# Later token groups of 512 by a quarter of the features, with block products of 256 columns, in a fused retention and feed-forward kernel

## The chip, the cores and the metric

One NeuronCore of a Trainium2 chip. The metric is the device time of one launch in microseconds (us), median over runs. All data is float32 except the two weight matrices, which arrive as float64 bit patterns and are converted on the core.

## What is computed

The reference, cut to what matters:

```python
# q, k, v: (4, 8, 768, 64); w_in: (512, 2048); w_out: (2048, 512)
for t in range(S):                                   # retention, per batch and head
    state = gamma * state + outer(k[t], v[t])
    y[t] = (q[t] @ state) / sqrt(D)
x = y.transpose(0, 2, 1, 3).reshape(3072, 512)
h = x @ w_in
sp = np.maximum(h, 0.0) + np.log1p(np.exp(-np.abs(h)))   # softplus
g = h * erf(sp)
out = g @ w_out                                      # (3072, 512)
```

## The kernel before

The order of all work is written out by hand in one Python function; every engine executes its own instructions in that order, and waits on semaphores where an operand or a buffer is not ready.

**Retention.** The 3072 tokens are 24 chunks j of 128 tokens (6 per batch). `load(j)` issues a chunk's DMAs on the SP queue: one for k, 16 small ones that put q into blocks of 32 by 32, 16 more that put k into such blocks (`kb`, `load_blocks`, L187), one for v. `prepared(j)` scales k, `kb` and q on VectorE (DVE) and transposes the blocks on DVE into `kT` and `qT`, in five steps. `sub_visit(j, g)` does the chunk's matmuls on TensorE (PE): scores against the masked keys, values, state, and the update of `state`; it writes the chunk's columns of `xT`. The pool `loads` has three buffers for `kq` and `v`, two for `kb`.

**First 512 tokens.** For these (g = 0 to 3, `G0` is 4) the hidden layer is computed plainly in groups of 512 tokens by 512 features while the weights are being loaded and converted (`weights`, `conversion`).

**Later groups.** From g = 4 to 23 the tokens go in pieces of 256, each with two groups of half the features. The first of them, `hidden_plain`, multiplies plainly. The other 19 use a fast block scheme for the hidden layer: x and `w_in` are cut into 4 blocks along the inner dimension, x into 2 blocks of 128 tokens, `w_in` into blocks of 256 features (4 per half); 26 products (`STEPS`) of sums of blocks give the 8 output blocks. The sums of x are made by 18 DVE additions (`x_sums`), the sums of `w_in` once per half by 30 DVE additions (`W_SUMS`, `sum_in`). `hidden_steps` executes a product as two matmuls of 128 columns (tokens), L951, into one of four PSUM banks, which the next steps use again in turn; each of 26 reads adds a bank into the output `h` in SBUF, the first write of a block by a copy on ScalarE (ACT), L965 and L967, the rest by DVE, L963.

The gate: softplus on ACT (`gate_softplus`), erf on ACT (`gate_erf`, another table), product with `h` on DVE (`gated`). The second layer uses a fast scheme of seven products (`project_part`, parts 1 to 7, L1034; four sums of `e` blocks, `g_sums`; sums of `w_out` blocks, `sums`, made by an ACT copy and an accumulating DMA from the POOL queue, L352 and L353). Its accumulators in four PSUM tiles `o0` to `o3` add up over the two groups of a token piece, and `put_part` then combines them into `r` and writes 256 rows of the output.

**Order within a later group.** During the 26 steps of group g, three parts of the second layer of group g-1 are put among them; after them stand softplus, a chunk's visit, the x sums of the next piece, `load(j+3)`, erf, four more parts of g-1, and the gate:

```python
        for n, _ in enumerate(hidden_steps(g), start=1):
            ...
            if n in (14, 18, 24):
                project_part(g - 1, {14: 1, 18: 2, 24: 4}[n])
        ...
            if even:
                all_of(prepared(j + 2))
            if j + 3 < NJ:
                load(j + 3)
            j += 1
        gate_erf(g)
        for p in (5, 6, 7, 3):
            project_part(g - 1, p)
```

Of the kernel before, what the change touches and what calls it, by code (L numbers as in the profile page):

```python
# [45 lines left out]
W_SUMS = (  # L46
    (16, 2, 6, "+"),
    (17, 8, 10, "-"),
    (4, 4, 17, "+"),
    (10, 10, 16, "+"),  # L50
    (18, 16, 4, "-"),
    (19, 18, 5, "-"),
    (20, 1, 19, "-"),
    (20, 0, 20, "+"),
    (21, 9, 20, "+"),
    (9, 13, 9, "-"),
    (22, 15, 13, "-"),
    (23, 15, 9, "-"),
    (7, 3, 7, "+"),
    (24, 20, 12, "-"),  # L60
    (25, 18, 7, "+"),
    (2, 2, 3, "+"),
    (8, 12, 8, "-"),
    (12, 17, 12, "-"),
    (3, 3, 15, "-"),
    (15, 2, 15, "-"),
    (19, 19, 13, "-"),
    (16, 16, 7, "+"),
    (7, 7, 10, "+"),
    (4, 4, 6, "-"),  # L70
    (1, 1, 5, "+"),
    (5, 5, 2, "+"),
    (6, 14, 12, "+"),
    (6, 6, 15, "-"),
    (13, 23, 11, "-"),
# [61 lines left out]
def kernel(  # L137
# [29 lines left out]
    loads = ctx.enter_context(tc.tile_pool(name="loads", bufs=3))  # L167
# [24 lines left out]
    def load(j):  # L192
        b, c = divmod(j, NC)
        if j == JPC - 1:

            x = act.tile([P, N], F32, name="e", bufs=1)
            KQ[j] = x[:, : 2 * d_model].rearrange("p (i h d) -> p i h d", i=2, h=H)
            V[j] = x[:, 2 * d_model : 3 * d_model].rearrange("p (h d) -> p h d", h=H)
        else:
            KQ[j] = loads.tile([P, 2, H, D], F32, name="kq")  # L200
            V[j] = loads.tile([P, H, D], F32, name="v")
        now = slice(c * C, (c + 1) * C)
        if j >= NB:
            KB[j] = loads.tile([P, HP * C], F32, name="kb", bufs=2)
            nc.sync.dma_start(KQ[j][:, 0], k[b, :, now, :].rearrange("h p d -> p h d"))
            load_blocks(KQ[j][:, 1].rearrange("p h d -> p (h d)"), q[b, :, now, :])
            load_blocks(KB[j], k[b, :, now, :])
# [14 lines left out]
    w_in_sb = const.tile([P, 2, N_W, 2 * P], F32, name="w_in_sb")  # L222
    w_out_sb = const.tile([P, 2, 7, FG, DH], F32, name="w_out_sb")

    def w_in_of(ft, kk):
        half, s, i = ft // (2 * FG), ft % (2 * FG) // FG, ft % FG
        return w_in_sb[:, s, 4 * (2 * half + i // 2) + kk, i % 2 * P : (i % 2 + 1) * P]

    def w_out_of(ft):
        half, s, i = ft // (2 * FG), ft % (2 * FG) // FG, ft % FG  # L230
        return w_out_sb[:, s, 2 * half : 2 * half + 2, i, :]
# [3 lines left out]
    CE = 2 * d_model  # L235
    spare = [w_out_sb[:, s, 4:7].rearrange("p a b c -> p (a b c)") for s in range(2)]
    spare += [w_in_sb[:, s, 16:24].rearrange("p a f -> p (a f)") for s in (1, 0)]
    raws = [x[:, : 2 * CE].bitcast(I64) for x in spare]

    def halves(x):  # L240
        return x.rearrange("p (h c) -> p h c", h=2).bitcast(U32)

    numbers = halves(spare[0][:, 2 * CE :])
    later = ret.tile([P, N_X, P], F32, name="xs", bufs=1)[:, : CE // P].rearrange("p a f -> p (a f)")
    powers = [halves(spare[1][:, 2 * CE :]), halves(later)]
    last_power = halves(spare[1][:, :CE])
# [38 lines left out]
    def conversion(n):  # L285
# [4 lines left out]
        half, s, at = i // 4, i % 4 // 2, i % 2  # L290
# [3 lines left out]
            range(2) if n < 4 else (None,), (slice(1), slice(1, 2)) if n == 0 else (slice(None),)  # L294
        )
        for part, rows in parts:
            last = n > 0 or rows.start == 1
            words = raws[place[n]].bitcast(U32)
            if which == "in":
                f = slice(2 * P) if part is None else slice(part * P, (part + 1) * P)  # L300
                fb = 2 * half + at
                to = w_in_sb[:, s, 4 * fb : 4 * fb + 4, f].rearrange("p (h k) f -> p h k f", h=2)
            else:
                to = w_out_sb[:, s, 2 * half : 2 * half + 2, at * 2 : at * 2 + 2, :]
            words = words.rearrange("p (h a b w) -> p h a b w", h=2, a=2, w=2)
            number, power = (
                x.rearrange("p h (q a b) -> p q h a b", q=1 if part is None else 2, a=2)[:, part or 0]
                for x in (numbers, last_power if n == n_p - 1 else powers[n % 2])
            )
            if part is not None:  # L310
                words, number, power, to = words[:, rows, :, f], number[:, rows], power[:, rows], to[:, rows]
# [26 lines left out]
    in_sums = [0, 0]  # L338

    def sum_in(s, upto):  # L340

        assert all(("hidden", 2 * FG + s * FG + u) in done for u in range(FG))
        for to, a, b, sign in W_SUMS[in_sums[s] : upto]:
            nc.vector.tensor_tensor(w_in_sb[:, s, to], w_in_sb[:, s, a], w_in_sb[:, s, b], op=OP[sign])
        in_sums[s] = max(in_sums[s], upto)

    def sums(s):

        assert ("project", s) in done
        x = {name: w_out_sb[:, s, at] for name, at in OUT.items()}  # L350
        for to, a, b in (("T1", "12", "11"), ("T2", "22", "T1"), ("T3", "22", "12"), ("T4", "21", "T2")):
            nc.scalar.activation(x[to], x[b], AF.Copy, scale=-1.0)  # L352
            nc.gpsimd.dma_start(x[to], x[a], accum_op=ALU.add)  # L353
            done.add((to, s))
# [17 lines left out]
    def later_sums():  # L372
        for s in range(2):
            yield from sums(s)
# [13 lines left out]
    def need(*what):  # L388
        nonlocal room
        while what not in done:  # L390
            if next(weight_steps, done) is done:
                next(last_steps)
# [38 lines left out]
    state_2 = loads.tile([P, HP * C], F32, name="kb", bufs=2)[:, : HP * D]  # L431
    state_2 = state_2.rearrange("p (u d) -> p u d", d=D)
    mid = [state, state_1, state_2, state, None, state_1]
    adds_of = {JPC: range(2), JPC + 1: range(1), JPC + 2: range(1)}
# [131 lines left out]
    def ret_mask(j):  # L566
        AM[j] = ret.tile([P, 2, HP, C], F32, name="am")
# [64 lines left out]
    def sub_mask(j):  # L632
        AM[j] = ret.tile([P, 2, HP, C], F32, name="am")
        for s in range(2):
            nc.vector.tensor_tensor(
                AM[j][:, s, :, :D],
# [30 lines left out]
    def sub_results(j):  # L667
# [4 lines left out]
        pp = [ret_psum() for _ in range(2)]  # L672
        for a in range(2):
            t, before = slice(a * D, (a + 1) * D), mid[2 * (j - JPC) + a]
            for u in PAIRS:
                for r in range(2):
# [3 lines left out]
                        start=(a == 0 and u % 2 == 0), stop=False, skip_group_check=True,  # L680
                    )

        for crossed in range(2):
            for u in PAIRS:
                for a in range(2):
# [6 lines left out]
                        AM[j][t, r, u, :D],  # L692
                        start=False, stop=True, skip_group_check=True,
                    )
        for r in range(2):
            nc.scalar.copy(XC[m][:, r::2, i * C : (i + 1) * C], pp[r][:, :2, :])
# [3 lines left out]
    def sub_sums(j):  # L700
        m, i = divmod(j, JPC)
        for r in range(2):
            a = 1 - r
            x = XC[m][:, r::2, i * C + a * D : i * C + (a + 1) * D]
            nc.vector.tensor_tensor(x, x, SC[j][a][:, 2:, :D], op=ALU.add)
# [7 lines left out]
    def sub_visit(j, g):  # L713
# [16 lines left out]
        def of_state(a):  # L730
            t = slice(a * D, (a + 1) * D)
            for u in PAIRS:
                for r in range(2):
                    col, own = u // 2, slice(r * D, (r + 1) * D)
                    x = state_1 if g == G0 else state
                    nc.tensor.matmul(  # L736
                        pp[r][col * D : (col + 1) * D, u % 2, t], x[own, u, :], QT[j][own, u, t],
# [7 lines left out]
        def of_values(crossed):  # L745
            for u in PAIRS:
                for a in range(2):
# [6 lines left out]
                        AM[j][t, r, u, :D],  # L754
# [5 lines left out]
        last = chunk_of(g - 1)  # L760
        if (g - G0) % 2 == 1:
            clear.update((("o", 0), ("o", 1)))
        new = [
            None if g == G0 else O[last][3][:, 1, :].rearrange("p (u d) -> p u d", d=D),
            pp[1][:, 2:, :].rearrange("p a (b d) -> p (a b) d", d=D),
        ]
        adds = range(int(g == G0), 2 if c < NC - 1 else 1)
# [8 lines left out]
        if g > G0 and c:  # L776
            nc.vector.tensor_tensor(state, state, new[0], op=ALU.add)
        elif g > G0:
# [17 lines left out]
        if c < NC - 1:  # L796
            nc.vector.tensor_tensor(state, state_1 if g == G0 else state, new[1], op=ALU.add)
# [12 lines left out]
    HS, E, O = {}, {}, {}  # L810

    def gate_softplus(g):


        name = "r" if g < 4 and g % 2 else "e"
        E[g] = act.tile([P, N], F32, name=name, bufs=1)
        nc.scalar.activation(E[g], HS[g], AF.Softplus)  # L817
# [6 lines left out]

    def gate_erf(g):

# [512 lines left out]
```

## Time and profile before

| what | value |
|---|---|
| time, three runs | median 663.42 us (663.25 to 664.19) |
| profiled execution | 663.2 us, of which the recorded span is 661.5 us |
| PE matmul busy | 655.3 us, 6200 instructions |
| PE weight loads busy | 556.6 us |
| DVE busy | 508.4 us, 1101 instructions |
| ACT busy | 280.1 us, 402 instructions |
| POOL busy | 11.5 us, 29 instructions |
| mean granted TensorE clock | 0.999 of full speed |
| first stretch, weights and first 512 tokens | to about 127.5 us |
| one later group, table load to table load (L1256) | 25.92 us, for instance 400.82 to 426.74 |

The profile is of one execution. Matmuls are pipelined, so their recorded lengths overlap; the distance of their starts is what they cost. Each float32 matmul appears as two passes with a weight load (PEld) each. DVE, ACT and POOL execute one instruction after another, and the distance of starts in a row is a little less than an instruction's recorded length. SPq and POOLq rows are the issuing of DMAs, not the transfers.

### The profile page before, as it was taken

How to read it: one execution, taken by the hardware profiler on the slowest of the kernel's cores; microseconds unless marked ns; L12 is line 12 of the kernel's file. 1: busy time of each engine (PE TensorE's matmuls, PEld its weight loads, DVE VectorE, ACT ScalarE, POOL GpSimd, SP SyncE). 2: the span in 40 equal slices, each digit the busy share in tenths (PEclk: the TensorE clock that was granted, in tenths of full speed). 3: DMA queues.
4: the chain of work that ended last, by engine and by line, in shares of the span. 5: the costliest groups of instructions: out<-in, count | busy, mean ns of one | idle time of the engine just before them, and what ended most of it. 6: DMA issues, size and time to landing. Idle time of an engine off the chain costs nothing.

```text
span 661.5 us, 15245 instructions
## 1 busy us (share of the span) xinstructions
PE 655.3 (99%) x6200; PEld 556.6 (84%) x6200; DVE 508.4 (77%) x1101; ACT 280.1 (42%) x402; POOL 11.5 (2%) x29
## 2 busy tenths in 40 slices
PE   8999999999999999999999999999999999999998
PEld 7744444576999999999999999999999999999997
DVE  5999999969986886787678678677787788476464
ACT  3468363445535334244254253342432442542440
POOL 1000000110100000000000000000000000000000
PEclk9999999999999999999999999999999999999999
DMA  9999944385753321222222322222231210000001
GB/s 189 222 244 212 247 130 106 63 152 91 145 122 61 85 46 34 66 47 46 69 45 47 73 40 47 61 51 43 41 75 35 45 54 1 2 34 0 1 33 33
DMA packets 159414, 51.90 MB, mean 78 GB/s; under 512 B 143216, under 2 KB 149744, under 8 KB 159344
## 3 DMA queue, kind: packets, MB, share of 16 engines
q1 hardware_dynamic: 157776, 46.72, 32.9%
q0 software_dynamic: 1152, 4.19, 3.3%
q8 instruction: 49, 0.80, 0.5%
q14 instruction: 21, 0.17, 0.1%
q10 hardware_dynamic: 416, 0.01, 0.0%
HBM read 40.39 MB, written 6.29 MB: 71 GB/s over the span
## 4 chain that ended last, share of the span: by engine, by line
PE 98%; DMA 1%; DVE 0%; SPq 0%; ACT 0%; issue 0%
PE o L1034 37%; PE hp L951 22%; PE r L951 12%; PE hp L860 8%; PE o L896 8%; PE hp L980 2%; PE r L736 2%; PE hp L628 1%; PE o L772 1%; DMA kq<-in_k_dram 1%; PE r L557 1%; PE o L604 1%; PE r L751 1%; PE hp L751 1%; PE r L524 1%; PE r L772 0%
## 5 line engine op out<-in xcount | busy, mean ns | idle before, releaser
L1034 PE MATMUL o<-w_out_sb,h 128*128 128x256 f32 (+1 forms) x648 | 143.8, 379 | 0.4 <-DVE r L1294 0.4
L951 PE MATMUL hp<-xs,w_in_sb 128*128 128x128 f32 x988 | 138.1, 275 | 0.0
L1034 PEld LDWEIGHTS o<-w_out_sb,h 128*128 128x128 f32 x648 | 120.5, 190 | 17.1 <-DVE r L1294 0.6
L963 DVE TENSOR_TENSOR h<-h,hp 128x256 f32<-128x256 f32 x190 | 78.0, 419 | 70.2 <-PE hp L951 65.4
L951 PEld LDWEIGHTS hp<-xs,w_in_sb 128*128 128x128 f32 x988 | 128.4, 192 | 2.9
L1034 PE MATMUL o<-w_out_sb,e 128*128 128x256 f32 x480 | 113.5, 379 | 0.0
L1034 PEld LDWEIGHTS o<-w_out_sb,e 128*128 128x128 f32 x480 | 86.8, 190 | 9.4
L817 ACT ACTIVATE e<-h 128x2048 f32<-128x2048 f32 x22 | 42.1, 1911 | 119.8 <-DVE h L963 119.7
L963 DVE TENSOR_TENSOR h<-h,r 128x256 f32<-128x256 f32 x152 | 56.9, 416 | 22.3 <-PE r L951 21.4
L965 ACT COPY h<-hp 128x256 f32<-128x256 f32 x38 | 14.2, 373 | 130.8 <-PE hp L951 102.6
L951 PE MATMUL r<-xs,w_in_sb 128*128 128x128 f32 x456 | 63.3, 275 | 0.0
L951 PEld LDWEIGHTS r<-xs,w_in_sb 128*128 128x128 f32 x456 | 57.0, 192 | 0.0
L860 PE MATMUL hp<-xT,w_in_sb 128*128 128x512 f32 (+2 forms) x144 | 56.5, 548 | 0.0
L849 DVE TENSOR_TENSOR e<-h,e 128x1024 f32<-128x1024 f32 x42 | 49.3, 1214 | 8.0 <-ACT e L830 8.0
L860 PEld LDWEIGHTS hp<-xT,w_in_sb 128*128 128x128 f32 x144 | 25.7, 190 | 27.0 <-issue 24.4
L951 PE MATMUL hp<-xT,w_in_sb 128*128 128x128 f32 x304 | 46.3, 275 | 0.0
L951 PEld LDWEIGHTS hp<-xT,w_in_sb 128*128 128x128 f32 x304 | 41.5, 192 | 1.4 <-issue 0.5
L830 ACT ACTIVATE e<-e 128x2048 f32<-128x2048 f32 (+1 forms) x23 | 42.1, 1836 | 0.2
L967 ACT ACTIVATE h<-hp 128x256 f32<-128x256 f32 x57 | 21.8, 383 | 29.6 <-PE hp L951 28.3
L951 PE MATMUL r<-xT,w_in_sb 128*128 128x128 f32 x228 | 31.7, 275 | 0.0
L830 ACT ACT_TABLE_LOAD x24 | 30.8, 1283 | 0.4
L951 PEld LDWEIGHTS r<-xT,w_in_sb 128*128 128x128 f32 x228 | 28.5, 192 | 0.0
(160 smaller groups left out, 794.8 us busy)
## 6 DMA issues: line engine op xcount, KB each, us to landing
w_out_sb<-in_moe_w_out_dram SPq DMA_DIRECT2D x14, 512.0 KB, 5.8
kq<-in_k_dram SPq DMA_DIRECT2D x23, 256.0 KB, 4.2
v<-in_v_dram SPq DMA_DIRECT2D x23, 256.0 KB, 3.5
out_dram<-r SPq DMA_DIRECT2D x23, 256.0 KB, 2.4
kq<-in_q_dram SPq DMA_DIRECT2D x288, 16.0 KB, 1.8
kb<-in_k_dram SPq DMA_DIRECT2D x288, 16.0 KB, 1.7
w_in_sb<-in_moe_w_in_dram SPq DMA_DIRECT2D x8, 512.0 KB, 12.4
w_out_sb<-w_out_sb POOLq DMA_DIRECT2D x8, 512.0 KB, 5.2
```

The lines of the kernel that those rows point to most:

```text
L736: nc.tensor.matmul(pp[r][col * D : (col + 1) * D, u % 2, t], x[own, u, :], QT[j][own, u, t], start=first(r, col), stop=True, skip_group_ch ...
L751: nc.tensor.matmul(other[a][own, u % 2, D:] if crossed else pp[a][own, u % 2, t], V[j][t, 2 * u + r, :], AM[j][t, r, u, :D], start=crossed ...
L817: nc.scalar.activation(E[g], HS[g], AF.Softplus)
L830: nc.scalar.activation(E[g][:, half], E[g][:, half], AF.Erf)
L849: nc.vector.tensor_tensor(E[g][:, half], HS[g][:, half], E[g][:, half], op=ALU.mult)
L860: nc.tensor.matmul(HP_[ft][:, t], w_in_of(ft, kk), XC[0][:, kk, t], start=(kk == 0), stop=(kk == n_k - 1),)
L896: nc.tensor.matmul(O[0][tt].rearrange("p (d c) -> p d c", d=2), E[g][:, u * TCH + tt * P : u * TCH + (tt + 1) * P], w_out_of(ft), start=(f ...
L951: nc.tensor.matmul(to[:, u, :], w_in_sb[:, s, w, u * P : (u + 1) * P], XS[m](x), start=first and u == 0, stop=True, skip_group_check=True,)
L963: nc.vector.tensor_tensor(h, h, of, op=ALU.add if plus else ALU.subtract)
L965: nc.scalar.copy(h, of)
L967: nc.scalar.activation(h, of, AF.Copy, scale=-1.0)
L1034: nc.tensor.matmul(O[m][i][:, half, at], G[g][a][:, u * P : (u + 1) * P], w_out_sb[:, s, OUT[b], u, at], start=i not in started, stop=(s = ...
```

## The change

Later groups become 512 tokens by a quarter of the features (512): 20 groups again (g = 4 to 23), four for each of the five blocks of 512 tokens. A product of the block scheme is one matmul with 256 tokens as its columns and 128 features as its rows; the first later group uses the scheme too, and `hidden_plain` is gone. The weights are laid out by quarters; the 30 sums of `w_in` are made four times, for the first quarter on DVE (`sum_in`), for the other three by ACT copies and accumulating DMAs from POOL (`sums_in`), put between other work by `some(1)` after every odd step, and what is left of the next quarter's sums is put out at the end of a group. The order of `W_SUMS` is another one.

The second layer of a group goes in two pairs of 128-token blocks (`pairs`, in alternating order): the first pair among the steps of the next group, the second between that group's visit and the next group's steps. The accumulators of a pair are drained after one or two groups (`results`), five times per block, and what is not the first write of its rows is added into the output in DRAM by an accumulating DMA from POOL; for one pair of the last block an SBUF tile collects the parts. Gate, softplus and erf go by pairs too.

To make room in SBUF, `loads` has two buffers instead of three, the load after a visit is `load(j+2)` instead of `load(j+3)`, and several tiles of the first stretch share memory with `e_all` and `xs`. Chunks 6 and 7 are handled ahead of the first later group, chunks 8 to 23 by visits, one in each of the first 16 groups.

The diff, cut to its core:

```diff
-    loads = ctx.enter_context(tc.tile_pool(name="loads", bufs=3))
+    loads = ctx.enter_context(tc.tile_pool(name="loads", bufs=2))
...
+    def sums_in(q):
+
+        ready_to_sum(q)
+        for to, a, b, sign in W_SUMS:
+            if to == a and sign == "-":
+                nc.vector.tensor_tensor(w_in_at(q, to), w_in_at(q, a), w_in_at(q, b), op=OP[sign])
+            else:
+                if sign == "-" or to not in (a, b):
+                    nc.scalar.activation(w_in_at(q, to), w_in_at(q, b), AF.Copy, scale=float(sign + "1"))
+                    b = a
+                elif to == b:
+                    b = a
+                nc.gpsimd.dma_start(w_in_at(q, to), w_in_at(q, b), accum_op=ALU.add)
+            in_sums[q] += 1
+            yield
...
     def later_sums():
-        for s in range(2):
-            yield from sums(s)
+        yield from sums_in(1)
+        yield from sums(0)
+        yield from sums_in(2)
+        yield from sums(1)
+        yield from sums_in(3)
...
         for w, x, bank, first, reads in STEPS:
-            to = banks[bank]
-            for u in range(2):
-                nc.tensor.matmul(
-                    to[:, u, :],
-                    w_in_sb[:, s, w, u * P : (u + 1) * P],
-                    XS[m](x),
-                    start=first and u == 0,
-                    stop=True,
-                    skip_group_check=True,
-                )
-            of = to[:, :2].rearrange("p u t -> p (u t)")
+            to = banks[bank][:, :SCH]
+            nc.tensor.matmul(to, w_in_at(q, w), XS[m](x), start=first, stop=True, skip_group_check=True)
+            of = to.rearrange("p (h c) -> p h c", h=2)
...
+    def results(g, pair):
+
+        m = block_of(g)
+        t0 = m * TCH + pair * SCH
+        r = act.tile([P, 8, DH], F32, name="r", bufs=1)
+        nc.scalar.copy(r[:, 7], OP_[pair][3][:, 0])
+        yield
+        nc.vector.tensor_tensor(
+            r[:, 0:5:4], OP_[pair][0], r[:, 7:8].to_broadcast([P, 2, DH]), op=ALU.add
+        )
+        yield
+        o57 = OP_[pair][1]
+        nc.vector.tensor_tensor(
+            r[:, 5:7], o57, r[:, 4:5].to_broadcast([P, 2, DH]), op=ALU.add
+        )
+        nc.vector.tensor_tensor(r[:, 3], r[:, 6], o57[:, 0], op=ALU.add)
+        yield
+        nc.vector.tensor_tensor(r[:, 1:3], r[:, 5:7], OP_[pair][2], op=ALU.add)
...
+            if t0 in written_out:
+                nc.gpsimd.dma_start(rows, x, accum_op=ALU.add)
+            else:
+                nc.sync.dma_start(rows, x)
...
+    sub_states(j + 1)
+    sum_in(0, len(W_SUMS) // 2)
+    project(G0 - 1, 1)
+    put_first(0)
+    some(4)
+    sub_results(j + 1)
+    sub_sums(j + 1)
+    x_sums(1)
+    load(j + 3)
+    sum_in(0, len(W_SUMS))
+    project(G0 - 1, 2)
+    put_first(1)
...
+    gate_softplus(G0)
+    project(G0 - 1, 3)
+    put_first(2)
+    sub_visit(j, ps_o.tile([P, 2, DH], F32, name="o0"))
+    put_first(3)
+    load(j + 2)
...
     for g in range(G0 + 1, NG):
...
+        next_chunk = prepared(j + 1) if more else none()
+        order = {
+            1: (next_chunk,), 2: (gated_x, late), 3: (gated_x,), 4: (next_chunk, late), 5: (late,), 6: (next_chunk, late),
+            7: (gated_y, late), 8: (next_chunk,), 9: (gated_y,), 10: (next_chunk,),
+            11: (sums_x,), 12: (sums_x,), 13: (sums_x,), 14: (sums_x,),
+            18: (sums_y,), 20: (sums_y,), 22: (sums_y,), 24: (sums_y,),
+        }
+        parts = {14: (1,), 16: (2,), 18: (4, 6), 20: (5,), 22: (7,), 24: (3,)}
+        drains = {15: 1, 19: 1, 23: 1, 25: 1}
         for n, _ in enumerate(hidden_steps(g), start=1):
             for steps in order.get(n, ()):
                 next(steps, None)
+            for p in parts.get(n, ()):
+                project_part(before, x, p)
+            if n in drains:
+                if n == 15:
+                    bank = OP_[x][3]
+                next(drain, None)
+            if n % 2:
+                some(1)
...
+        if g + 1 < NG and quarter(g + 1):
+            while in_sums[quarter(g + 1)] < len(W_SUMS):
+                next(last_steps)
 
         nc.scalar.activation(idle, idle, AF.Softplus)
-        gate_softplus(g)
+        gate_softplus(g, x)
         if more:
-            sub_visit(j, g)
+            sub_visit(j, bank)
+            if j + 2 < NJ:
+                load(j + 2)
             j += 1
+        for p in (1, 2, 4):
+            project_part(before, y, p)
+        gate_softplus(g, y)
+        if g + 1 < NG and quarter(g + 1) == 0:
+            x_sums(block_of(g + 1))
+        for p in (6, 5, 7, 3):
+            project_part(before, y, p)
+        if at == FG - 1:
+            late = results(before, y)
+        if g < NG - 1:
+            for pair in pairs(g):
+                gate_erf(g, pair)
```

In the texts below, group 0 is the first later group (g = 4), group 1 the next, up to group 19; a link is one step of a chain of dependent weight sums.

## The prediction

> **What bounds the kernel now.** First the page: engine shares and the chain that ended last.
>
> ```profile
> span 661.5 us, 15245 instructions
> ...
> PE 655.3 (99%) x6200; PEld 556.6 (84%) x6200; DVE 508.4 (77%) x1101; ACT 280.1 (42%) x402; POOL 11.5 (2%) x29
> ...
> PE 98%; DMA 1%; DVE 0%; SPq 0%; ACT 0%; issue 0%
> ```
>
> TensorE is the bound from end to end, and nobody makes it wait. So two questions decide: is its own work less afterwards, and does anything begin to hold it up? Second, the timeline of a later group (columns: start, length, engine, line, operation).
>
> ```profile
> 425.26 0.61 PE L951 MATMUL hp<-xs,w_in_sb 128*128 128x128 f32 x4
> ...
> 425.71 0.61 PE L951 MATMUL hp<-xT,w_in_sb 128*128 128x128 f32 x4
> ...
> 434.17 0.46 PE L736 MATMUL r<-qT,state 64*64 64x64 f32 x16
> ...
> 447.90 0.69 DVE L537 TENSOR_TENSOR kq<-kq,kq_s 128x512 f32<-128x512 f32 x1
> ...
> 448.50 1.41 DVE L963 TENSOR_TENSOR h<-h,r 128x256 f32<-128x256 f32 x4
> ...
> 449.45 1.89 PE L1034 MATMUL o<-w_out_sb,e 128*128 128x256 f32 x8
> ...
> 451.18 0.61 PE L951 MATMUL hp<-xs,w_in_sb 128*128 128x128 f32 x4
> ```
>
> The profile counts two passes per matmul. Take starts, not lengths: four 128-column passes start every 0.445 us, 0.111 each; eight 256-column passes take 451.18-449.45 = 1.73, 0.2165 each. Twice 0.111 is 0.222: PE is limited by columns, and 256 columns in one instruction save 0.006 us of 0.222. DVE in a row: four 256-column additions in 1.41 us, 0.335 each with the last at its full 0.42; the 512-column step starts 0.60 before the next; 128 columns take 0.21 (five of L933 in 1.10).
>
> Third, the SP queue in that group, the sizes and landings on the page, and the accumulating DMA of the second-layer weights.
>
> ```profile
> 435.12 0.39 SPq L205 DMA_DIRECT2D kq<-in_k_dram  x1
> 435.56 9.01 SPq L187 DMA_DIRECT2D kq<-in_q_dram  x16
> 444.62 7.54 SPq L187 DMA_DIRECT2D kb<-in_k_dram  x16
> ```
>
> ```profile
> kb<-in_k_dram SPq DMA_DIRECT2D x288, 16.0 KB, 1.7
> ...
> w_out_sb<-w_out_sb POOLq DMA_DIRECT2D x8, 512.0 KB, 5.2
> ```
>
> ```profile
> 164.61 0.85 POOL L353 DMA_DIRECT2D w_out_sb<-w_out_sb  x1 [10.06 <-ACT w_out_sb L352]
> ...
> 170.44 2.01 ACT L352 ACTIVATE w_out_sb<-w_out_sb 128x1024 f32<-128x1024 f32 x2 [2.68 <-DMA w_out_sb<-w_out_sb]
> ```
>
> One chunk's load starts 0.96 us after the last block product (434.16) and its last `kb` piece is issued at 452.16: landed at 453.9, 19.7 us after that product. The accumulating DMA holds its follower 170.44-164.61 = 5.8 us.
>
> **TensorE's own work.** Removed: 19 groups x 104 passes x 0.1113 = 219.9, and `hidden_plain`, 64 x 0.2165 = 13.9. Added: 20 x 52 x 0.2165 = 225.2. Second layer: 56 passes a group on both sides. Sum -8.6 us. The Trainium skill (Perfetto Trace Analysis, Matmuls) says larger matmuls are more efficient when possible; its TensorE: Matmul & The Clock Gate (Back-to-back issue gap) gives sustained spacings of 81 ns at 128 columns and 131 at 512, by which 256 columns would cost far less than two of 128 and the block products nearly halve, an estimate of some -90 us. The two starts above decide against it: 0.2165 against 0.222.
>
> **The load of a chunk.** Before, with three buffers, `load(j+3)` follows the visit of chunk j, and the chunk is scaled more than a group later. Now two buffers, `load(j+2)` after the visit, and `prepared(j+1)` of the next group's block products wants that very chunk. The built program's DVE order in a group is: k scale, two 512-column gates, `kb` scale, then the first addition into h (step 5). The `kb` scale waits for all 16 pieces. From the end of a group's block products (0): visit 2.0, seven parts of the second pair 28 x 0.2165 = 6.06, so step 1 could start at 8.06 and step 5's result is there at 10.4. `kb` lands at 19.7. Steps 1 to 8 run; step 9 needs bank 0 again, which the addition of step 5, queued behind the `kb` scale, reads at 20.3; step 9 starts at 20.8 instead of 11.5: 9.3 lost. Then DVE has, from the `kb` scale to the addition of step 13, six 512-column steps (3.65) and ten of 256 columns (9 x 0.335 + 0.42), so bank 0 is free for step 15 only at 26.85; PE lacks another 2.6 on the way there. From there 12 steps x 0.433 and 6 parts x 0.866 = 10.4: the group ends at 37.2. Without waits it is 25.4; before, the table loads of L1256 stand 25.92 apart. Lost: 11.9 a group. In the second quarter of a block the left-over drain puts 2.13 us of DVE work into the same stretch: 14.0. This meets groups 4 to 14 (eight regular, three with the drain): 95 + 42 = 137 us. Group 3 is loaded during an earlier stall and loses only the DVE part, 2.3; the last five, without chunks, 4.7.
>
> The price's ends: if the pieces land at 17, 9.2 a group; if the drain of SP is as in the slowest load (383.34 to 401.1), 12.7.
>
> **PE's clock.** In the stretch from 658.0 to 661.5, where PE does 0.64 us of work, the granted clock reads 0.80; nothing longer is seen. A wait of 9 us may thus lower it. TensorE: Matmul & The Clock Gate (What's actually happening) puts the idle clock at half after about 3.4 us, for about as long; by it an estimate of 1.7 us a group; no run here shows it. By the rows: were steps 9 to 13 (5 x 0.433) to take twice as long, the 2.2 us would fit into the 2.6 that PE then waits for DVE anyway. I take 0, and 11 x 2.2 = +24 as the upper end.
>
> **Weight sums by DMA.** Quarter 0 costs DVE 30 x 0.21. Quarters 1 to 3 each become 25 accumulating 64 KB DMAs, 16 ACT copies and 5 DVE steps. For such a DMA the trace has no row: lower end 0.85 + 1.7 (POOL step and 16 KB landing) = 2.55, upper end the 5.8 of 512 KB; I take 3.2, nearer the small end, as 64 KB is an eighth (out_dram: 64 KB lands in 1.6, 256 KB in 2.4). DMA: Bandwidth & Descriptors (Anatomy of one DMA) states 2.0 us plus bytes/436e3, an estimate of 2.15; no row here has that size. With 0.27 per ACT copy and 0.3 to POOL, the longest dependent chain of the 30 sums is 37 us; from sum 8 to the end 30, from 14 to the end 23. ACT and DVE take their queues in order, so whatever stands behind a waiting copy waits too:
> - Start. `prepared(7)` waits for chunk 7's `kb` (135.9 + 1.7 = 137.6); four DVE steps, masks, 15 sums, `x_sums` (18 x 0.335 = 6.0), 5 sums end at 153.9. PE's own work (from 127.5: two begins and two results at 1.1, three parts at 3.5) ends at 142.4: 11.5.
> - Group 0: block-product copies behind copies of quarter 1: 3.4. Then the four second-layer sums with two 5.8 us links hold ACT: first copy at 165, two links of 7.2 (1.06 + 0.3 + 5.8), last copy, table and softplus 1.06 + 1.28 + 1.91 end at 183.7, the copies into `xT` behind them let group 1 start at 185.8 instead of 174.5: 11.3.
> - Group 1: its chunk's load stands on SP behind `put_first(3)`, starts at 186.5, lands at 205.2; step 9 at 206.3: 19.7 with the first waits. At its end 16 sums of quarter 2 are put out at once ahead of softplus, and their last DVE steps ahead of the visit's state addition: sum 8 is issued at step 15, the chain ends 30.2 later and the state addition 0.7 after it, while PE comes to wait for that state 10.4 + 1.8 after step 15: 19.
> - Group 2: four second-layer sums among the first steps hold ACT (step 8 starts at 9.7 instead of 3.0, step 14 at 16.9 instead of 5.6; part of it is waited for anyway): 9.8. At its end 21 sums of quarter 3 at once, the state at 54.2 from the group's start, PE waiting for it at 31.4: 22.8.
> Sum 97.5 (with 2.55 per DMA 83, with 5.8 about 140).
>
> **The rest.** Five drains per block instead of two: 15 more x 2.13 us of DVE, in the stretches above. Additions into DRAM on POOL: two per drain, 26 in all at 0.85; the buffer `r` comes round 20 us later at the soonest, so they are hidden (if not, ACT's first drain copy waits for up to 5.8). The end: 84 passes instead of 88, but the last pair is gated after the first: +1.
>
> **Sum.** 663.2 (the profiled execution; span 661.5, median of the runs 663.42) - 8.6 + 97.5 + 2.3 + 137 + 4.7 + 1 = 897; I say 895.
>
> **Rivals.**
> 1. The load does not bind: `kb` lands before 10 us, or DVE's queue is not blocked by it. Then regular groups lose DVE's own crowding, 2.3 (drain 4.2, `x_sums` 3.6): 41 in all, and the start and the sums some 75: 770. For it: before, DVE waits for `kb` once only, 3.0 us. Against: that load has a group more time.
> 2. Everything added is hidden, and only PE's columns count: 663.2 - 8.6 = 655, faster. It decides if SP gives a chunk's 32 pieces in under 9 us (16.6 above) and a DMA link costs under 1 us. DVE's 77% leaves room on average, but a wait in order is no matter of averages.
> 3. Slower still: DMA links of 5 us and a halved clock after each wait: 940 and more.
> The change does what it says: the built program has 520 block products of 256 columns.
>
> **Numbers.** Forecast 0.66 (its own range 840 to 945), rival 1 and what lies between it and the forecast 0.22, rival 2 0.05, rival 3 0.07. About 0.2% is what a measurement can tell from no change. Range 770 to 945: it leaves out rival 2, most of 3 and the low tail of 1. Faster 0.04, same 0.01, slower 0.95.
>
> **What would show it.** Right: table loads about 37 us apart in groups 4 to 14 and 26 in the last ones; DVE waiting about 10 us a group for `kb`'s DMA; PE waiting for DVE's addition into h; two PE holes of about 20 us at the ends of groups 1 and 2 with ACT and DVE waiting for `w_in` DMAs; 256-column passes 0.2165 apart. Wrong: `kb` waits under 3 us a group, or PE at 98% of the chain.

## The result and the profile after

| | median, us | range |
|---|---|---|
| before | 663.42 | 663.25 to 664.19 |
| after, four runs | 915.81 | 913.56 to 916.64 |

The changed kernel takes 1.3796 times as long (95% interval 1.3768 to 1.3823). The forecast was 895, its own range 840 to 945. The profiled execution took 913.56 us, 250.4 us more than that of before; its page opens so:

```profile
span 911.9 us, 13667 instructions
...
PE 704.0 (77%) x5196; PEld 543.9 (60%) x5196; DVE 536.3 (59%) x1200; ACT 297.5 (33%) x501; POOL 102.2 (11%) x130
...
PE 35%; SPq 20%; DVE 16%; DMA 13%; issue 11%; ACT 3%; POOL 2%; DVEq 0%; ACTq 0%; POOLq 0%
```

Nothing is busy four fifths of the time, so waits, not work, set the time: the chain that was PE's at 98% now runs a fifth of its length through the issuing of DMAs on SP. The waits (engine, line, what for: us in total, times, longest) name the places:

```profile
PE hp L1006 <- DVE h L1012: 131.5, 27, 13.4
DVE kb L584 <- DMA kb<-in_k_dram: 123.0, 13, 11.9
...
PE r L785 <- DVE state L823: 37.1, 2, 21.2
```

The first two lines are in the main one and the same stall, seen from two engines: DVE waits for the pieces of `kb` (L584), and PE for the addition into `h` (L1012) that stands behind that step in DVE's queue. The third line is the two holes ahead of the state additions. Next the timeline of group 10:

```profile
569.35 7.87 SPq L187 DMA_DIRECT2D kq<-in_q_dram  x16
577.26 7.54 SPq L187 DMA_DIRECT2D kb<-in_k_dram  x16
...
577.45 0.60 PE L1006 MATMUL r<-xT,w_in_sb 128*128 128x256 f32 x2
...
586.27 0.69 DVE L584 TENSOR_TENSOR kb<-kb,kq_b 128x512 f32<-128x512 f32 x1 [10.34 <-DMA kb<-in_k_dram]
586.88 0.41 DVE L1012 TENSOR_TENSOR h<-h,hp 128x256 f32<-128x256 f32 x1
...
587.35 2.08 PE L1006 MATMUL hp<-xs,w_in_sb 128*128 128x256 f32 x4 [9.30 <-DVE h L1012]
...
593.33 0.70 PE L1006 MATMUL hp<-xs,w_in_sb 128*128 128x256 f32 x2
```

The block products of the group before ended at 566.1. From there: `kb` is scaled at 20.2 (forecast: landing at 19.7), step 8 is the row at 577.45, step 9 starts at 21.2 (20.8), step 15 at 27.2 (26.85). PE's wait is 9.30, the forecast 9.3.

Behind the wait, too, the four passes of the row at 587.35 take 2.08 us, about twice 1.03, which four take elsewhere in the group: the granted clock reads 0.50 from 587.3 to 589.2 and 1.00 again from 593.3 on. Where the 250.4 us arose follows from the starts of the softplus tables, one per group (L1321 after, L1256 before):

| stretch | before | after | more | forecast, with its share of the -8.6 |
|---|---|---|---|---|
| start to the table of group 3 | 219.62 | 323.49 | 103.9 | 96.2 |
| to that of group 14 (11 groups) | 284.6 | 425.6 | 141.0 | 133.5 |
| to that of group 19 | 127.2 | 127.2 | 0.0 | 3.1 |
| to the end of the span | 30.1 | 35.6 | 5.5 | 1 |

The forecast's share of PE's own work is -2.6 for group 0 and -0.32 for each later one, so the first row is 97.5 + 2.3 - 3.6 and the second 137 - 3.5.

### The profile page after: what moved, and what is told of

The parts are those of the page before. It is cut to its first block, busy times and chain, and to the rows that moved or that the text cites. A ratio compares the mean times of both kernels' runs of the same rounds, so it can differ in the third digit from the quotient of the medians.

```text
span 911.9 us, 13667 instructions
## 1 busy us (share of the span) xinstructions
PE 704.0 (77%) x5196; PEld 543.9 (60%) x5196; DVE 536.3 (59%) x1200; ACT 297.5 (33%) x501; POOL 102.2 (11%) x130
## 4 chain that ended last, share of the span: by engine, by line
PE 35%; SPq 20%; DVE 16%; DMA 13%; issue 11%; ACT 3%; POOL 2%; DVEq 0%; ACTq 0%; POOLq 0%
SPq L187 18%; PE o L1066 14%; PE hp L1006 12%; PE r L1006 5%; DMA kq<-in_q_dram 4%; DVE h L1012 4%; DMA kb<-in_k_dram 3%; DVE xs L994 1%; DVE e_all L1028 1%; DMA w_in_sb<-w_in_more 1%; DMA kq<-in_k_dram 1%; POOL w_in_sb L374 1%; DMA w_in_more<-w_in_more 1%; DMA w_in_more<-w_in_sb 1%; PE o L953 1%
## 5 line engine op out<-in xcount | busy, mean ns | idle before, releaser
L1006 PE MATMUL hp<-xs,w_in_sb 128*128 128x256 f32 x360 | 122.0, 454 | 134.6 <-DVE h L1012 131.5
L1006 PEld LDWEIGHTS hp<-xs,w_in_sb 128*128 128x128 f32 x360 | 75.5, 224 | 164.5 <-DVE h L1012 150.5
L1012 DVE TENSOR_TENSOR h<-h,hp 128x256 f32<-128x256 f32 x200 | 82.8, 415 | 77.7 <-PE hp L1006 70.2
L584 DVE TENSOR_TENSOR kb<-kb,kq_b 128x512 f32<-128x512 f32 x18 | 12.4, 690 | 123.0 <-DMA kb<-in_k_dram 123.0
L1066 PE MATMUL o<-w_out_sb,e_all 128*128 128x256 f32 x304 | 81.1, 402 | 0.0
L1028 DVE TENSOR_TENSOR e_all<-h,e_all 128x512 f32<-128x512 f32 x76 | 50.4, 685 | 47.0 <-ACT e_all L876 47.0
L1066 PE MATMUL o<-w_out_more,h 128*128 128x256 f32 x312 | 76.8, 379 | 0.0
L1066 PE MATMUL o<-w_out_sb,h 128*128 128x256 f32 x312 | 76.8, 379 | 0.0
L1012 DVE TENSOR_TENSOR h<-h,r 128x256 f32<-128x256 f32 x160 | 62.9, 413 | 7.2 <-ACT h L1016 3.4
L1066 PEld LDWEIGHTS o<-w_out_sb,e_all 128*128 128x128 f32 x304 | 59.8, 201 | 9.5
L1066 PEld LDWEIGHTS o<-w_out_sb,h 128*128 128x128 f32 x312 | 59.4, 190 | 7.9
L1066 PEld LDWEIGHTS o<-w_out_more,h 128*128 128x128 f32 x312 | 59.4, 190 | 7.9
L1006 PE MATMUL hp<-xs,w_in_more 128*128 128x256 f32 x160 | 46.4, 393 | 0.2 <-ACT h L1014 0.2
L785 PE MATMUL r<-qT,state 64*64 64x64 f32 x480 | 14.8, 232 | 37.1 <-DVE state L823 37.1
## 6 DMA issues: line engine op xcount, KB each, us to landing
w_in_more<-in_moe_w_in_dram SPq DMA_DIRECT2D x8, 512.0 KB, 11.6
```

Of the source, the lines that this page charges most:

```text
L584: nc.vector.tensor_tensor(x, x, by, op=ALU.mult)
L785: nc.tensor.matmul(pp[r][col * D : (col + 1) * D, u % 2, t], state[own, u, :], QT[j][own, u, t], start=first(r, col), stop=True, skip_grou ...
L1006: nc.tensor.matmul(to, w_in_at(q, w), XS[m](x), start=first, stop=True, skip_group_check=True)
L1012: nc.vector.tensor_tensor(h, h, of, op=ALU.add if plus else ALU.subtract)
L1028: nc.vector.tensor_tensor(e[:, own], h[:, own], e[:, own], op=ALU.mult)
L1066: nc.tensor.matmul(acc[i][:, half, at], G[g, pair][a][:, u * P : (u + 1) * P], w_out_at(q, OUT[b])[:, u, at], start=(pair, i) not in start ...
```

## The experiments

**1. Prepare the chunk late.** `late_prep` moves only the five steps of `next_chunk` within a group:

```diff
-            1: (next_chunk,), 2: (gated_x, late), 3: (gated_x,), 4: (next_chunk, late), 5: (late,), 6: (next_chunk, late),
-            7: (gated_y, late), 8: (next_chunk,), 9: (gated_y,), 10: (next_chunk,),
+            2: (gated_x, late), 3: (gated_x,), 4: (late,), 5: (late,), 6: (late,),
+            7: (gated_y, late), 9: (gated_y,),
...
-            18: (sums_y,), 20: (sums_y,), 22: (sums_y,), 24: (sums_y,),
+            17: (next_chunk,), 18: (sums_y,), 20: (sums_y,), 21: (next_chunk,), 22: (sums_y,),
+            23: (next_chunk,), 24: (sums_y,), 25: (next_chunk,), 26: (next_chunk,),
```

> The changed kernel with one edit: the five DVE steps that prepare the next chunk stand behind steps 17, 21, 23, 25 and 26 of a group's block products instead of 1, 4, 6, 8 and 10; the load itself starts where it did. Theory (the `kb` scale, waiting for 16 late pieces, blocks DVE's queue and with it bank 0): by step 19 the pieces are there, so the 9 to 10 us of waiting go in groups 4 to 14 and most of the 19.7 us in group 1; what stays is DVE's crowding of 2.3 us a group. Table loads 27 to 29 us apart in groups 4 to 14 instead of 37.4 to 40.7; time 775 to 810 us instead of 914. Rival 1 (the new block scheme with its DVE additions and drains is too much for DVE, the load only shows where DVE would be late anyway): the period stays above 34 us and the time above 880. Rival 2 (the clock that drops in each wait costs most): the same as the theory, since the waits go with it; told apart by the run with dummy matmuls.

791.03 us, 1.192 times before (1.190 to 1.194). Groups 4 to 14 take 319.0 us instead of 425.6, 29.0 each; groups 1 to 3 take 122.1 instead of 140.3. The waits of this run:

```profile
DVE kb L584 <- DMA kb<-in_k_dram: 2.3, 1, 2.3
...
PE hp L1006 <- DVE h L1012: 27.6, 35, 3.2
```

The 123.0 us of waiting for `kb` are 2.3, and PE's wait for L1012 falls from 131.5 to 27.6. Nothing else was moved: half of the loss, 125 of 252 us, came from the place of five steps in an in-order queue, of which the `kb` scale is the one that waited.

**2. The same stall, taken away at its source.** `one_dma` leaves DVE's order and shortens SP's work:

```diff
-        for s, d in itertools.product(range(2), range(2)):
...
+        nc.sync.dma_start(to.rearrange("p (h d) -> p h d", h=H), src.rearrange("h p d -> p h d"))
```

> The changed kernel with the order of all DVE steps as it is, but each chunk's q and `kb` come by one DMA of 256 KB each instead of 16 of 16 KB; the values are then not in blocks of 32 by 32, so the output is not the reference's. SP issues a chunk in about 2 us instead of 17. Theory (the 32 issues on SP set when `kb` lands): `kb` lands some 6 to 7 us after the end of a group's block products instead of 19.7, ahead of step 5, so the wait on its DMA is under 1 us a group; table loads 27 to 29 us apart in groups 4 to 14; time 775 to 815 us, about that of the kernel with the preparation moved. Rival (DVE's crowding or the order of its steps costs, not the landing): period above 34, time above 880.

793.72 us (1.194 to 1.198 times before): as late_prep. The SP row and the wait:

```profile
437.18 0.58 SPq L184 DMA_DIRECT2D kq<-in_q_dram  x1
```

```profile
DVE kb L578 <- DMA kb<-in_k_dram: 1.4, 2, 0.8
```

One issue of 0.58 us stands where 16 took 7.87. Two different edits, one on DVE's order and one on SP, give 125 and 122 us: the stall is the product of a late landing and a queue in order, and either half removes it.

**3. The load's timing alone, in the kernel before.** `before_late` copies the changed kernel's calls:

```diff
-    load(j + 3)
+    load(j + 2)
...
+        order.update({n: (next_chunk,) for n in (1, 4, 6, 8, 10)})
```

> The kernel before with only the timing of its chunks changed to that of the changed kernel: `load(j+2)` after a visit instead of `load(j+3)`, and the chunk prepared in steps 1, 4, 6, 8 and 10 of the very next group; 256 by half the features, two matmuls of 128 columns, and all weight sums stay. Theory (the load is the main cost, and it needs nothing of the new scheme): per group the visit 2.0 and four parts 6.9 take PE to 8.9 us after its block products, steps 1 to 8 to 12.5, `kb` lands at 19.7 and step 9 starts at 20.8: 8.3 lost, and up to 2.6 more behind it, in 15 or 16 groups: 663 + 125 to 175, about 800 (785 to 840). Rival (the load costs only together with the new scheme's DVE work): under 690.

693.78 us (1.043 to 1.051 times before): neither. The timeline of this run shows why (the first two rows are the load, the last two the end of the block products and the visit):

```profile
501.15 0.41 SPq L205 DMA_DIRECT2D kq<-in_k_dram  x1
501.61 9.73 SPq L187 DMA_DIRECT2D kq<-in_q_dram  x16
...
505.48 0.61 PE L951 MATMUL hp<-xT,w_in_sb 128*128 128x128 f32 x4
506.02 0.46 PE L736 MATMUL r<-qT,state 64*64 64x64 f32 x16
```

The load starts 4.9 us before the visit (506.02) that it follows in the code: thanks to the third buffer SP hardly waits for PE (1.3 us in the whole run). What it did wait for is the output write ahead of it in SP's own queue (issued at 500.22; such writes wait 214.6 us for their results in this run, nine times), and right behind it come two chunks' loads in a row, at 501.15 and 519.52. The table loads then stand 25.7 to 25.9 and 27.8 to 31.6 us apart in turn, and `kb` is waited for eight times, 29.1 us in all. `before_two` takes the third buffer away:

```diff
+            two = j >= JPC + 4
+            KQ[j] = KQ[j - 2] if two else loads.tile([P, 2, H, D], F32, name="kq")
+            V[j] = V[j - 2] if two else loads.tile([P, H, D], F32, name="v")
```

> The run before_late gave 693.8, not 800: its load(j+2) starts while the block products still run (SP at 501.15, the products end at 505.9), because the third buffer is still there and SP, a queue of its own, waits for no visit. So the order of the calls is not the cause; the buffer is. This run is the same kernel, but from chunk 8 on each chunk's `kq` and `v` take the tiles of the chunk two before, so two buffers in effect. Theory (the load starts when the visit frees the buffer, `kb` lands 19.7 us after the products, PE is back at step 1 after 8.9): 8.3 to 11 us lost in each of some 15 groups, 663 + 125 to 165: 785 to 830. Rival (the buffer doesn't matter, the waits of `kb` in every second group are all that the early preparation costs): 690 to 705.

829.72 us (1.247 to 1.257 times before). Its SP and PE rows, and its waits:

```profile
509.47 0.46 PE L737 MATMUL r<-qT,state 64*64 64x64 f32 x16
510.49 0.39 SPq L206 DMA_DIRECT2D kq<-in_k_dram  x1
```

```profile
DVE kb L547 <- DMA kb<-in_k_dram: 155.3, 17, 11.3
PE hp L952 <- DVE h L964: 128.1, 16, 9.4
```

Now the load follows the visit, and SP waits for the visits' matmuls 14 times, 182.8 us in all. The former kernel, with its 128-column products and its own weight sums, loses 166 us: 30 by the later call and the early preparation together, 136 more by the missing buffer. The stall owes nothing to the block products of 256 columns.

**4. The weight sums on DVE.** `sums_dve` replaces the copies and accumulating DMAs of quarters 1 to 3:

```diff
...
-                    nc.scalar.activation(w_in_at(q, to), w_in_at(q, b), AF.Copy, scale=float(sign + "1"))
...
-                nc.gpsimd.dma_start(w_in_at(q, to), w_in_at(q, b), accum_op=ALU.add)
+            nc.vector.tensor_tensor(w_in_at(q, to), w_in_at(q, a), w_in_at(q, b), op=OP[sign])
```

> The changed kernel with one edit: the sums of `w_in` of quarters 1 to 3 are made by DVE additions (30 x 0.21 us each) in the same places, instead of ACT copies and accumulating DMAs; the second-layer sums stay as they are. Theory (the chain of links of 3 us holds ACT, DVE and the state): the two PE holes of 15 to 20 us ahead of the state additions of groups 1 and 2 go, for 3.4 and 4.4 us of DVE additions at the ends of these groups, and the copies of group 0 stop delaying: 915 - 45 + 9 = 879, range 865 to 892. Groups 4 and later unchanged at 37 to 40 us. Rival (these holes only stand in front of other waits, of the load or of the second-layer sums): over 905.

888.34 us (1.334 to 1.341 times before), inside the range, 9 above the sum. The holes are gone:

```profile
PE r L777 <- DVE state L815: 6.3, 2, 3.7
...
DVE kb L576 <- DMA kb<-in_k_dram: 138.2, 16, 11.7
```

37.1 us of waiting for the state fell to 6.3, but the waits for `kb` rose from 13 to 16 and by 15 us: group 3, whose load had run during the hole of group 2 (23.0 us from table to table), now takes 38.1. Part of a gain came back as another stall.

**5. Both, and then the second-layer sums too.** `late_sums` is late_prep and sums_dve in one; `late_sums_all` also changes `sums`:

```diff
-            nc.scalar.activation(x[to], x[b], AF.Copy, scale=-1.0)
-            nc.gpsimd.dma_start(x[to], x[a], accum_op=ALU.add)
+            nc.vector.tensor_tensor(x[to], x[a], x[b], op=ALU.subtract)
```

> Both edits at once: the preparation late, and the sums of `w_in` of quarters 1 to 3 by DVE. Theory (two separate causes that add): 791 less the 27 us that the sums gave alone, and some more because no wait for `kb` in group 1 covers them any longer: 745 to 768. Rival (the holes ahead of the state additions are replaced by other waits): above 780.

> As late_sums, and the eight second-layer sums are DVE subtractions too (8 x 1.2 us) instead of ACT copies and accumulating DMAs of 512 KB. Theory (their two links of 7 us hold ACT: 11.3 us in group 0, 9.8 in group 2): 10 to 20 us below late_sums, 730 to 750. What is then left above the 655 of the columns is the start (11.5), DVE's crowding in groups with a chunk (3.5 x 12) and DVE's own sums. Rival (ACT has room there, the links are hidden): within 4 us of late_sums.

769.45 and 760.36 us (1.157 to 1.161 and 1.142 to 1.147 times before). 791.03 less the 27.5 of sums_dve would be 764, so the two causes add to within 6 us, 1 above the range given. The second-layer sums are worth 9 us, just under the 10 to 20 expected, and the time itself lies 10 above the 730 to 750. The 97 us that late_sums_all lies above before: 55 up to the table of group 3, 35 in groups 4 to 14 (29.0 us each), 2 up to group 19, 5.5 at the end. So more than half of the 103.9 us ahead of that table stays although no weight sum goes by DMA any more: 29 of the 55 lie ahead of group 1's table, 16 and 10 in the two groups after it (37.7 and 35.6 us from table to table, 21.2 and 25.9 before). The state additions are still waited for there (2.84 and 3.85 us); how the rest divides was not isolated.

**6. Is it the clock?** `warm` puts dummy matmuls ahead of step 9:

```diff
+            for _ in range(warm if n == 8 else 0):
+                nc.tensor.matmul(
+                    banks[1][:, SCH:], w_in_at(q, w), XS[m](x), start=False, stop=True, skip_group_check=True
+                )
```

> The changed kernel with 18 dummy matmuls of 256 columns (36 passes, 7.8 us) ahead of step 9 of each group whose next chunk was loaded in the group before, into a part of a bank that nobody reads; they end before the 9.3 us of the wait are over, so PE does not idle long. Theory of the prediction (the halved clock after the wait is absorbed, since DVE frees bank 0 for step 15 no earlier): table loads of groups 4 to 14 at most 0.6 us closer than in the changed kernel, 0 to 6 us in all: 908 to 915. Rival (the 19 us by which the sum came out too low are the clock's): 1.2 to 2.2 us a group, 890 to 902.

930.29 us (1.400 to 1.404 times before): outside both, but the timeline answers the question.

```profile
593.38 7.93 PE L1006 MATMUL hp<-xs,w_in_sb 128*128 128x256 f32 x36
...
602.51 1.13 PE L1010 MATMUL hp<-xs,w_in_sb 128*128 128x256 f32 x4 [1.21 <-DVE h L1016]
...
608.49 0.70 PE L1010 MATMUL hp<-xs,w_in_sb 128*128 128x256 f32 x2 [1.52 <-DVE h L1016]
```

After the dummies the four passes of steps 9 and 10 take 1.13 us; in the changed kernel, after 9.30 us without work, they took 2.08 (its row at 587.35). The granted clock reads 1.00 here (602.5 to 603.6) and 0.50 there (587.3 to 589.2). So the wait halves the clock, and the dummies prevent it. Yet step 15 starts 5.98 us after step 9 in both (608.49 - 602.51, 593.33 - 587.35): the slow passes only fill time in which PE at full clock waits for DVE, the 1.52 us of the last row; with the slow passes the row at 593.33 has no such wait. The rule of the Trainium skill that the prediction weighed (TensorE: Matmul & The Clock Gate, What's actually happening) has the half clock right; how long a wait it takes is another matter (last section), and the estimated 1.7 us a group is not on the path here. The longer time comes from elsewhere: 2.7 us up to group 2, 8.0 in group 3, which had no wait for `kb` to fill, and 7.5 in groups 4 to 14 (3.9 of them in groups 4 to 7, 2.5 in group 13). In the whole run `kb` was waited for 129.3 instead of 123.0 us; why its pieces come later was not settled.

**7. The columns.** `split` is late_sums_all with two matmuls of 128 columns for each block product:

```diff
+                nc.tensor.matmul(
+                    to[:, t], w_in_at(q, w), XS[m](x)[:, t],
+                    start=first and not t.start, stop=True, skip_group_check=True,
+                )
```

> The kernel late_sums_all (760 us) with each block product as two matmuls of 128 columns again instead of one of 256, nothing else. Theory (PE is limited by columns, so the change's own idea gains only 0.006 us in 0.222): four passes every 0.445 us instead of two every 0.433, at most 1040 x 0.006 = 6 us more, part of it hidden in DVE's waits: 760 to 767. Rival (a larger matmul is the cheaper one, as the sustained spacings of the Trainium skill, TensorE: Matmul & The Clock Gate, Back-to-back issue gap, would have it): four 128-column passes take clearly more than two of 256, and the time goes up by 30 us or more.

763.92 us (1.148 to 1.153 times before; late_sums_all 1.142 to 1.147). Starts in split, then in late_sums_all:

```profile
365.23 0.61 PE L999 MATMUL hp<-xs,w_in_sb 128*128 128x128 f32 x4
365.67 0.61 PE L999 MATMUL r<-xs,w_in_sb 128*128 128x128 f32 x4
```

```profile
382.06 0.59 PE L997 MATMUL r<-xs,w_in_sb 128*128 128x256 f32 x2
382.49 0.59 PE L997 MATMUL r<-xs,w_in_more 128*128 128x256 f32 x2
```

Four passes of 128 columns in 0.44 us, two of 256 in 0.43. What the change's name promises is worth 3.6 us, about as much as the runs of either kernel spread (3 to 4 us). The rule of the Trainium skill that larger matmuls are more efficient (Perfetto Trace Analysis, Matmuls) holds here to 2 or 3% of a product, far from the estimate of 90 us by the spacings.

**8. Less work on DVE.** `all_pool` moves the three scaling steps of a chunk to POOL:

```diff
+        on = nc.gpsimd if j > JPC + 5 else nc.vector
...
-            nc.vector.tensor_tensor(x, x, by, op=ALU.mult)
+            on.tensor_tensor(x, x, by, op=ALU.mult)
```

> The kernel late_sums_all with the three scaling steps of a chunk on POOL instead of DVE (behind steps 16 to 18; the transposes on DVE behind 25 and 26). Theory (what is left in groups with a chunk, 28.6 us against 25.9 before, is DVE's crowding): 3 x 0.6 = 1.8 us of DVE less in some 14 groups, up to 25 us: 735 to 750. Rival (the crowding is bound to the places where the additions into h and the gate stand, not to DVE's sum, or POOL takes long and the transposes wait for it): 755 to 775.

761.25 us (1.145 to 1.150 times before): nothing gained; the rival's side. The groups of instructions (busy us, mean ns) of all_pool, then of late_sums_all:

```profile
L576 POOL TENSOR_TENSOR kb<-kb,kq_b 128x512 f32<-128x512 f32 x14 | 14.7, 1051 | 168.8 <-DMA kb<-in_k_dram 158.1 <-DMA v<-in_v_dram 10.7
```

```profile
L1020 DVE TENSOR_TENSOR e_all<-h,e_all 128x512 f32<-128x512 f32 x76 | 55.3, 749 | 75.7 <-ACT e_all L868 75.7
```

```profile
L1019 DVE TENSOR_TENSOR e_all<-h,e_all 128x512 f32<-128x512 f32 x76 | 50.5, 685 | 76.0 <-ACT e_all L867 76.0
```

DVE was relieved of 42 steps, but its busy time in groups 4 to 14 fell only from 231.5 to 223.4 us, as other steps of it became slower (the gate by 64 ns an instruction on average; the last section shows which). These groups take 320.1 us instead of 319.2: the regular ones 28.2 on average after 28.0, those with a left-over drain 31.2 to 31.7 after 31.4 to 31.9. So this edit relieved DVE by little and is a weak test of its sum; whether what is left in these groups goes by the sum or by where the steps stand, no run here separates.

## Why the prediction was right, and where its sum was off

**PE's own work (-8.6).** Right as far as it is shown: block products start 0.43 apart, and `split` measures 3.6 of the 6 us that the wider products were to save. The last groups, without chunks, take on average 25.4 us on both sides; the 4.7 us of DVE work put down for them, less 1.6 of PE's saving, did not come.

**The load.** The main term, and right in mechanism and place: PE's wait in group 10 is 9.30 for a forecast of 9.3, and three groups with the drain take 40.3 to 40.7 us for 39.4. It was 7.4 us too small over groups 4 to 14, some 0.7 a group: `kb` is scaled half a microsecond later than the forecast had it land, and both restarts of PE (steps 9 and 15) are 0.4 late. One reason was incomplete. The prediction took the load's start from the call's place after the visit; before_late against before_two shows that, with the same call, the third buffer lets the load start ahead of the visit, and only without it SP waits for the visits. What stands ahead in SP's own queue counts too: group 10's load at 567.79 comes right behind an output write (566.84, 0.84 long).

**PE's clock, taken as 0.** The granted clock did fall, to 0.86 in group 10's stretch, but the value 0 was right in these groups, and for the reason given: step 15 starts 5.98 us after step 9 with either clock. Behind the two holes of the next paragraph the half clock may well cost something.

**The weight sums (97.5).** The whole stretch to group 3 is 7.7 us over the forecast. The link was forecast at 3.2; the 64 KB DMAs land in 3.0 (median of L374, 2.3 to 5.2), where the 2.15 estimated by the formula of the Trainium skill (DMA: Bandwidth & Descriptors, Anatomy of one DMA) is too low. The start was forecast at 11.5: between 127 and 160 us PE was busy for 21.4 of 33, 11.6 lost. That the numbers agree is partly luck, as half of it (5.4) is another wait than named, behind a sum on DVE that waits for its link, and the first block product starts at 156.9, not right behind 153.9. The two holes were forecast at 19 and 22.8:

```profile
242.43 0.71 PE L785 MATMUL r<-qT,state 64*64 64x64 f32 x16 [15.82 <-DVE state L823]
```

```profile
303.34 0.29 DVE L367 TENSOR_TENSOR w_in_sb<-w_in_sb 128x128 f32<-128x128 f32 x1 [19.44 <-DMA w_in_sb<-w_in_sb]
...
304.03 0.42 DVE L823 TENSOR_TENSOR state<-state,o 128x256 f32<-128x256 f32 x1
...
304.50 0.71 PE L785 MATMUL r<-qT,state 64*64 64x64 f32 x16 [21.23 <-DVE state L823]
...
305.14 3.76 PE L1066 MATMUL o<-w_out_sb,e_all 128*128 128x256 f32 x8
```

15.8 and 21.2, in the order that the prediction gave: the state addition (L823) stands behind a sum (L367) that waits for its chain. What the sum left out is the last row: after such a hole the second pair's parts run at half the clock (0.53 from 304.4 to 309.0), eight passes in 3.76 us against 1.89 in a row at full clock. That is 1.8 us of start to start, and here PE's next wait comes only 17 us later (1.52 us at 321.93). The first hole has the same (3.78 us at 243.06), but group 2's waits for ACT behind it (5.24 us at 260.31) may hide it. The rest of the 7.7 (group 1 starting at 187.6 instead of 185.8 among it) was not isolated. How the 97.5 divides is borne out only in part: DVE sums for both kinds of weights and the late preparation take 49 of the 103.9 back, and 55 stay in late_sums_all.

**The rest.** The 26 additions into DRAM are hidden but for one ACT wait of 6.1 us. The end was 4.5 too small: the second pair's gate starts at 898.82, right behind the last step of the first pair's drain on DVE (898.23), and PE waits for it until 899.65, 1.67 us; the forecast had +1, and the other waits of the end were not taken apart.

**The rivals.** Rival 1 was a load that does not bind with all else as forecast: late_prep and one_dma make that case, and it is 791 and 794, not 770, so its price was low by what the forecast missed outside the load's stretches and by DVE's crowding (late_prep's groups 4 to 14 lie 34 us above before, where 2.3 and 4.2 a group make 31). Rival 2, columns alone, is refuted by the result, and neither of its conditions holds: SP needs 15.4 us for a chunk's 32 pieces (7.87 + 7.54 in group 10) and a link takes 3.0. Rival 3 asked for links of 5 us and a clock that counts after each wait; the links are 3.0, and after the waits for `kb` the clock does not count.

## What to carry to other kernels

Follow a removed buffer to the queue that fills it, and from there to the first instruction that waits for the data: with three buffers the 17 us of small DMAs on SP ran ahead unseen, with two they began after the last use, and one scaling step at the front of an in-order queue turned that into 9 to 12 us of TensorE waiting in each group. Before a stall is designed around, ask whether its consumer could simply stand later; that recovered 125 of the 252 us with no other edit. And measure the promised gain in the trace before paying for it: two starts in the profile of before already told that 256 columns in one instruction are worth almost nothing over two of 128.

## What the runs showed of the hardware

A wait of 2.84 us (late_sums_all, at 217.94) was followed by eight passes in 3.58 us instead of 1.73, at a granted clock of 0.50. After one of 1.98 us in the same run (at 192.12) the first passes went at the full rate, and the half clock came only 1 us later: 1.00 from 192.1 to 193.1, 0.52 from 193.1 to 196.5, with four passes in 1.71 us instead of 0.87 from 194.63 on. One of 1.67 us ahead of 899.65 in the changed kernel was followed by passes at the full rate (1.00 up to 905). So the half clock comes after waits well short of the 9 us that the prediction worried about, and it can come late: the passes right behind a wait do not tell.

While POOL did 128x512 tensor steps (1.05 to 1.22 us each on average, where DVE takes 0.69), DVE's gate went from 685 to 749 ns on average. The mean hides most of it. In groups 4 to 14 of all_pool a DVE step with both inputs in SBUF that met a running POOL step ended 0.27 to 0.56 us after that step, however short it is by itself; the others took what they always take. The gate step at 442.66, beside a POOL step from 442.68 to 444.39, took 2.29 us and ended at 444.95; a 256-column step at 419.86 took 0.67 instead of 0.42, ending 0.27 after POOL's step (420.26). Additions with one input in PSUM beside a POOL step (364.98, 392.67) took 0.42 as ever. The Trainium skill says in its GPSIMD Engine Reference, Specifications, that POOL shares its SBUF interfaces with VectorE and contends with steps of two SBUF inputs; this trace agrees.
